# Reordering the transfers at a fused kernel's start, and moving its normalisation pieces within the FFN stages

## Chip, cores, metric

One core of a Trainium2 chip. The metric is device time in microseconds. Each time is the median of a kernel's runs, and the kernel before was run beside every new kernel on the same chip. "Span" is the time from the first to the last instruction of the profiled run; it is 1 to 2 us less than the time. In the profile lines PE is TensorE, PEld its weight loads, DVE VectorE, ACT ScalarE, POOL GpSimd, SP SyncE, and a bracket holds the idle time before an instruction and what ended it. The granted clock is the share of its full rate at which TensorE was let run.

## The reference, cut to what matters

```python
# retention: batch 4, 8 heads, 768 steps, head_dim 64
for t in range(S):
    state = gamma * state + outer(k[:, :, t], v[:, :, t])
    y[:, :, t] = scale * q[:, :, t] @ state
x = y.transpose(0, 2, 1, 3).reshape(3072, 512)
# RMS norm and SwiGLU FFN, d_ff 1536
xn = x / sqrt(mean(x * x) + 1e-6) * rms_g
out = (silu(xn @ w_gate) * (xn @ w_val)) @ w_out
```

## The kernel before

The 768 steps are cut into six chunks of 128. While the FFN of chunk c runs in 16 slots (12 gate/value blocks `gv`, then 4 `down` blocks), the attention pieces of chunk c+1 are put between the slots. Program order is kept on every engine. The chunk's 512 token rows (4 batches of 128) must all have passed through `piece_x` before the next FFN can start.

```python
    for b in range(B):
        load(0, b)                # q, k, v of chunk 0: 12 transfers of 256 KB on SP
    # ... constants, g_bc on SP ...
    for i in range(DFF // WB):    # weights: 8 + 3 transfers on GpSimd, cast to bf16
        nc.gpsimd.dma_start(out=wg_b[:, :, sl], in_=wg_v[:, :, sl])
        nc.gpsimd.dma_start(out=wv_b[:, :, sl], in_=wv_v[:, :, sl])
    # ... wo likewise, 3 transfers ...

    def cast(c, b):               # three GpSimd instructions, then load(c + 1, b)
    def piece_t(c, b):            # transposes of q, k (PE), qkT copy (ACT)
    def piece_a(c, b):            # scores (PE), causal mask am (DVE)
    def piece_y(c, b):            # y, kv (PE); x (DVE); xsq (ACT); state (DVE, POOL)
    def piece_rstd(c):            # once per chunk: two GpSimd instructions
    def piece_x(c, b):
        nc.vector.scalar_tensor_tensor(out=xn, in0=x, scalar=rstd, in1=g_bc, ...)
        for s in range(KS):
            nc.tensor.transpose(xt_ps[:, s, :], xn[:, s * 128:(s + 1) * 128], ident)
        nc.vector.tensor_copy(cur[c, "xnT"][:, :, b * C:(b + 1) * C], xt_ps)

    def attention(c):             # slot of each piece
        for b in range(B):
            s[2 * b].append(lambda b=b: cast(c, b))
            s[2 * b + 1].append(lambda b=b: piece_t(c, b))
            s[2 * b + 2].append(lambda b=b: piece_a(c, b))
            s[2 * b + 3].append(lambda b=b: piece_y(c, b))
            s[12 + b].append(lambda b=b: piece_x(c, b))
        s[10].append(lambda: piece_rstd(c))

    def gv(n):                    # 4 + 4 matmuls of 512 columns
        # g_ps, v_ps (PE), sg = Silu(g_ps) (ACT), hT = sg * v_ps (DVE)
```

Of the kernel before, what the change touches and what calls it, by code (L numbers as in the profile page):

```python
# [9 lines left out]
F32 = mybir.dt.float32  # L10
BF16 = mybir.dt.bfloat16
AX = mybir.AxisListType
AF = mybir.ActivationFunctionType
ALU = mybir.AluOpType
# [3 lines left out]
def kernel(  # L18
# [24 lines left out]
    lng = [math.log(1.0 - 2.0 ** (-5.0 - h)) for h in range(H)]  # L43

    const = ctx.enter_context(tc.tile_pool(name="const", bufs=1))
    loads = ctx.enter_context(tc.tile_pool(name="loads", bufs=5))
    work = ctx.enter_context(tc.tile_pool(name="work", bufs=3))
    ffw = ctx.enter_context(tc.tile_pool(name="ffw", bufs=3))
    aps = ctx.enter_context(tc.tile_pool(name="aps", bufs=4, space=bass.MemoryType.PSUM))
# [2 lines left out]

    out_v = out.rearrange("(b c p) m -> c b p m", b=B, p=C)


    raw = {}

    def load(c, b):
        t = []
        for name, src in (("q_f", q), ("k_f", k), ("v_f", v)):  # L60
            x = loads.tile([128, H, D], F32, name=name)
            nc.sync.dma_start(  # L62
                out=x, in_=src[b].rearrange("h (c p) d -> c p h d", p=C)[c])
            t.append(x)
        raw[c, b] = t

# [22 lines left out]
    for h in range(H):  # L89
        nc.scalar.activation(vdec[:, :, h], pos_f, AF.Exp, scale=-lng[h], bias=zero)  # L90
        nc.scalar.activation(ydec[:, :, h], pos_f, AF.Exp, scale=lng[h], bias=lnscale)
    eps4 = const.tile([128, B], F32, name="eps4")
    nc.gpsimd.memset(eps4, 1e-6)
    mhalf4 = const.tile([128, B], F32, name="mhalf4")
    nc.gpsimd.memset(mhalf4, -0.5)
    g_bc = const.tile([128, DM], F32, name="g_bc")
    nc.sync.dma_start(out=g_bc, in_=moe_rms_g.partition_broadcast(128))

# [11 lines left out]
    wv_v = moe_w_val.rearrange("(k p) n -> p k n", p=128)  # L110
    wo_v = moe_w_out.rearrange("(n p) m -> p n m", p=128)
    WB = 384
    for i in range(DFF // WB):
        sl = slice(i * WB, (i + 1) * WB)
        nc.gpsimd.dma_start(out=wg_b[:, :, sl], in_=wg_v[:, :, sl])
        nc.gpsimd.dma_start(out=wv_b[:, :, sl], in_=wv_v[:, :, sl])
    for i in range(3):
        sl = slice(i * 4, (i + 1) * 4)
        nc.gpsimd.dma_start(out=wo_b[:, sl, :], in_=wo_v[:, sl, :])


    cur = {}

    def cast(c, b):
        q_f, k_f, v_f = raw.pop((c, b))
        qb = work.tile([128, DM], BF16, name="qb")
        kb = work.tile([128, DM], BF16, name="kb")
        vp = work.tile([128, H, D], BF16, name="vp")
        nc.gpsimd.tensor_copy(qb, q_f.rearrange("p h d -> p (h d)"))  # L129
        nc.gpsimd.tensor_copy(kb, k_f.rearrange("p h d -> p (h d)"))  # L130
        nc.gpsimd.tensor_tensor(  # L131
            out=vp, in0=v_f, in1=vdec[:, c, :, None].to_broadcast([128, H, D]), op=ALU.mult)
        cur[c, b] = dict(qb=qb, kb=kb, vp=vp)
        if c + 1 < NCH:
            load(c + 1, b)

    def piece_t(c, b):
# [25 lines left out]
    def piece_y(c, b):  # L163
        d = cur[c, b]
        y_ps = aps.tile([128, H, D], F32, name="y_ps", tag="at")
        first = True
        for hp in range(NHP):
            for i in range(2):
                h = 2 * hp + i
                last = c == 0 and h == H - 1  # L170
                nc.tensor.matmul(y_ps[:, h, :], d["am"][:, i, hp, :], d["vp"][:, h, :],  # L171
                                 start=first, stop=last, skip_group_check=True)
                first = False
        if c > 0:
            for hp in range(NHP):
                nc.tensor.matmul(y_ps[:, 2 * hp:2 * hp + 2, :], d["qT"][:, hp, :], st_b[b][:, hp, :],
                                 start=False, stop=hp == NHP - 1, skip_group_check=True)
        if c < NCH - 1:
            kv_ps = aps.tile([128, NHP, 128], F32, name="kv_ps", tag="at")
            for hp in range(NHP):  # L180
                sl = slice(hp * 128, (hp + 1) * 128)
                nc.tensor.matmul(kv_ps[:, hp, :], d["kb"][:, sl],
                                 d["vp"][:, 2 * hp:2 * hp + 2, :], start=True, stop=True)
        x = work.tile([128, H, D], BF16, name="x", bufs=5)
        nc.vector.tensor_tensor(  # L185
            out=x, in0=y_ps, in1=ydec[:, c, :, None].to_broadcast([128, H, D]), op=ALU.mult)
        xsq = work.tile([128, DM], F32, name="xsq")
        nc.scalar.activation(xsq, x.rearrange("p h d -> p (h d)"), AF.Square,  # L188
                             accum_out=cur[c, "ssq"][:, b:b + 1])
        if c < NCH - 1:  # L190
            for i in range(2):
                r = slice(i * 64, i * 64 + 64)
                kv = kv_ps[r, :, i * 64:i * 64 + 64]
                if c == 0:
                    nc.vector.tensor_copy(st_f[b][r], kv)
                else:
                    nc.vector.tensor_tensor(out=st_f[b][r], in0=st_f[b][r], in1=kv, op=ALU.add)  # L197
                nc.gpsimd.tensor_copy(st_b[b][r, :, i * 64:i * 64 + 64], st_f[b][r])  # L198
        d["x"] = x

    def piece_rstd(c):
        ssq = cur[c, "ssq"]
        ms = work.tile([128, B], F32, name="ms")
        nc.gpsimd.tensor_scalar(out=ms, in0=ssq, scalar1=1.0 / DM, scalar2=1e-6,
                                op0=ALU.mult, op1=ALU.add)
        rstd = work.tile([128, B], F32, name="rstd")
        nc.gpsimd.tensor_tensor(out=rstd, in0=ms, in1=mhalf4, op=ALU.pow)  # L207
        cur[c, "rstd"] = rstd

    def piece_x(c, b):  # L210
        x = cur.pop((c, b))["x"]
        xn = work.tile([128, DM], BF16, name="xn")
        nc.vector.scalar_tensor_tensor(  # L213
            out=xn, in0=x.rearrange("p h d -> p (h d)"), scalar=cur[c, "rstd"][:, b:b + 1],
            in1=g_bc, op0=ALU.mult, op1=ALU.mult)
        xt_ps = aps.tile([128, KS, 128], BF16, name="xt_ps", tag="at")
        for s in range(KS):
            nc.tensor.transpose(xt_ps[:, s, :], xn[:, s * 128:(s + 1) * 128], ident)  # L218
        nc.vector.tensor_copy(cur[c, "xnT"][:, :, b * C:(b + 1) * C], xt_ps)  # L219

    def begin(c):
        cur[c, "ssq"] = work.tile([128, B], F32, name="ssq")
        cur[c, "xnT"] = work.tile([128, KS, GT], BF16, name="xnT", bufs=2)

    def attention(c):

        s = [[] for _ in range(16)]
        s[0].append(lambda: begin(c))
        for b in range(B):
            s[2 * b].append(lambda b=b: cast(c, b))  # L230
            s[2 * b + 1].append(lambda b=b: piece_t(c, b))
            s[2 * b + 2].append(lambda b=b: piece_a(c, b))
            s[2 * b + 3].append(lambda b=b: piece_y(c, b))
            s[12 + b].append(lambda b=b: piece_x(c, b))
        s[10].append(lambda: piece_rstd(c))
        return s


    def ffn(c):
        xnT = cur.pop((c, "xnT"))  # L240
        hT = ffw.tile([128, NFF, GT], BF16, name="hT", bufs=2)
        slots = []

        def gv(n):
            sl = slice(n * 128, (n + 1) * 128)
            g_ps = fps.tile([128, GT], F32, name="g_ps", tag="ff")
            for s in range(KS):
                nc.tensor.matmul(g_ps, wg_b[:, s, sl], xnT[:, s, :], start=s == 0, stop=s == KS - 1)  # L248
            v_ps = fps.tile([128, GT], F32, name="v_ps", tag="ff")
            for s in range(KS):  # L250
                nc.tensor.matmul(v_ps, wv_b[:, s, sl], xnT[:, s, :], start=s == 0, stop=s == KS - 1)  # L251
            sg = ffw.tile([128, GT], BF16, name="sg")
            nc.scalar.activation(sg, g_ps, AF.Silu)  # L253
            nc.vector.tensor_tensor(out=hT[:, n, :], in0=sg, in1=v_ps, op=ALU.mult)  # L254

        def down(b):
            o_ps = fps.tile([128, DM], F32, name="o_ps", tag="ff")
            for n in range(NFF):
                nc.tensor.matmul(o_ps, hT[:, n, b * C:(b + 1) * C], wo_b[:, n, :],  # L259
                                 start=n == 0, stop=n == NFF - 1)  # L260
            o_sb = ffw.tile([128, DM], F32, name="o_sb")
            nc.scalar.copy(o_sb, o_ps)  # L262
            nc.sync.dma_start(out=out_v[c, b], in_=o_sb)

        for n in range(NFF):
            slots.append(lambda n=n: gv(n))
        for b in range(B):
            slots.append(lambda b=b: down(b))
        return slots
# [5 lines left out]
    for c in range(NCH):  # L275
        f_slots = ffn(c)
        a_slots = attention(c + 1) if c + 1 < NCH else [[] for _ in range(16)]
        for i in range(16):
            f_slots[i]()
            for f in a_slots[i]:  # L280
                f()

# [29 lines left out]
```

## Time and profile before

A stage is the stretch from one FFN's first matmul (g_ps) to the next one's.

| kernel before | us |
|---|---|
| first FFN matmul | 59.26 |
| stage 0 (FFN 0, attention 1) | 42.99 |
| stages 1, 2, 3, 4 | 40.47, 40.52, 40.53, 40.30 |
| last stage (FFN 5 alone) | 35.33 |

One more view will be compared later: what TensorE waited for in stage 2 (142.72 to 183.24 us). Its columns are who waited, for whom, us in all, times, longest:

```profile
PE g_ps L248 <- DVE xnT L219: 0.5, 1, 0.5
PE y_ps L171 <- DVE am L158: 0.5, 3, 0.2
PE a_ps L154 <- ACT qkT L144: 0.3, 1, 0.3
```

So TensorE waits 1.3 us in a stage, never more than 0.52 us at a time. The first of these is the stage end, where xn and xnT of the last batch come behind the last down block.

### The profile page before, as it was taken

What the parts mean: (1) busy time and instruction counts of PE and PEld (TensorE: products, weight loads), DVE (VectorE), ACT (ScalarE), POOL (GpSimd) and SP (SyncE); (2) the same over time, 40 slices, a digit from 0 to 9 for tenths busy, and PEclk for the clock granted to TensorE, in tenths of its full rate; (3) what the DMA queues carried; (4) which work ended last, traced back from release to release, by engine and by line L of the source; (5) the groups of instructions that cost most, each with busy time, mean ns of one, the idle gap of its engine ahead of it and who ended that gap; (6) DMA issues with size and microseconds to landing.
All of it is one profiled execution on the core that took longest, in us unless ns stands there. A gap on an engine that the chain in (4) does not pass through costs nothing.

```text
span 299.4 us, 4437 instructions
## 1 busy us (share of the span) xinstructions
PE 242.3 (81%) x1696; PEld 122.8 (41%) x1696; DVE 141.1 (47%) x232; ACT 100.0 (33%) x186; POOL 91.2 (30%) x153
## 2 busy tenths in 40 slices
PE   0025212399999999999999999999999999999994
PEld 0014111145544454544454444545444444544441
DVE  0006405617765266873376653577544556424300
ACT  5012212034452245431445313544224453233321
POOL 8472245403337006281035350161921101000000
PEclk9999999999999999999999999999999999999999
DMA  8999999992400498002793025970110000110012
GB/s 164 191 191 192 196 197 227 219 218 44 96 3 35 129 228 171 2 0 105 182 225 53 0 73 137 219 136 1 36 71 36 2 0 2 70 70 2 1 47 93
DMA packets 84310, 30.43 MB, mean 102 GB/s; under 512 B 75457, under 2 KB 81089, under 8 KB 84289
## 3 DMA queue, kind: packets, MB, share of 16 engines
q1 hardware_dynamic: 78480, 25.43, 41.0%
q0 software_dynamic: 5808, 4.72, 9.8%
q8 instruction: 13, 0.21, 0.3%
q14 instruction: 9, 0.07, 0.1%
HBM read 28.57 MB, written 6.29 MB: 116 GB/s over the span
## 4 chain that ended last, share of the span: by engine, by line
PE 53%; DVE 17%; ACT 9%; SPq 8%; DMA 6%; issue 5%; POOL 1%; DVEq 0%; ACTq 0%; POOLq 0%
PE o_ps L259 21%; PE g_ps L248 13%; PE v_ps L251 12%; SPq L62 8%; DVE am L158 7%; DMA k_f<-in_k_dram 6%; DVE hT L254 4%; ACT xsq L188 3%; DVE x L185 3%; ACT qkT L144 3%; ACT sg L253 3%; PE xt_ps L218 2%; PE y_ps L171 2%; DVE xn L213 1%; DVE xnT L219 1%
## 5 line engine op out<-in xcount | busy, mean ns | idle before, releaser
L254 DVE TENSOR_TENSOR hT<-sg,v_ps 128x512 bf16<-128x512 bf16 x72 | 49.5, 688 | 72.5 <-PE v_ps L251 45.4
L248 PE MATMUL g_ps<-xnT,wg_b 128*128 128x512 bf16 x288 | 75.9, 387 | 3.1 <-DVE xnT L219 3.1
L251 PE MATMUL v_ps<-xnT,wv_b 128*128 128x512 bf16 x288 | 74.9, 383 | 0.0
L259 PE MATMUL o_ps<-wo_b,hT 128*128 128x512 bf16 x288 | 65.6, 379 | 0.0
L253 ACT ACTIVATE sg<-g_ps 128x512 bf16<-128x512 f32 x72 | 43.0, 597 | 63.9 <-PE g_ps L248 63.9
L198 POOL CAST st_b<-st_f 64x256 bf16<-64x256 f32 x40 | 15.9, 397 | 110.6 <-DVE st_f L197 102.5
L158 DVE TENSOR_TENSOR am<-a_ps,causal 128x512 bf16<-128x512 f32 x48 | 30.8, 682 | 33.5 <-PE a_ps L154 33.5
L251 PEld LDWEIGHTS <-wv_b 128*128 128x128 bf16 x288 | 28.5, 99 | 35.0 <-issue 1.7
L259 PEld LDWEIGHTS <-hT 128*128 128x128 bf16 x288 | 27.5, 98 | 30.4
L248 PEld LDWEIGHTS <-wg_b 128*128 128x128 bf16 x288 | 25.5, 99 | 29.1 <-DVE xnT L219 3.5
L262 ACT COPY o_sb<-o_ps 128x512 f32<-128x512 f32 x24 | 14.1, 586 | 56.5 <-PE o_ps L259 56.5
L144 ACT COPY qkT<-qk_ps 128x1024 bf16<-128x1024 bf16 x24 | 23.9, 998 | 25.0 <-PE qk_ps L142 25.0
L188 ACT ACTIVATE xsq<-x 128x512 f32<-128x512 bf16 x24 | 15.1, 630 | 49.4 <-DVE x L185 47.7
L142 PE MATMUL qk_ps<-ident,qb 128*128 128x128 bf16 x96 | 10.2, 234 | 24.4 <-POOL qb L129 24.4
L131 POOL TENSOR_TENSOR vp<-v_f,vdec 128x512 bf16<-128x512 f32 x24 | 26.8, 1117 | 8.7 <-DMA v_f<-in_v_dram 5.5
L219 DVE COPY xnT<-xt_ps 128x512 bf16<-128x512 bf16 x24 | 10.2, 425 | 31.4 <-PE xt_ps L218 31.4
L213 DVE SCALAR_TENSOR_TENSOR xn<-x,rstd,g_bc 128x512 bf16<-128x512 bf16 x24 | 23.5, 980 | 1.9 <-POOL rstd L207 1.9
L129 POOL CAST qb<-q_f 128x512 bf16<-128x512 f32 x24 | 17.0, 707 | 14.4 <-issue 8.8
L171 PE MATMUL y_ps<-vp,am 128*128 128x64 bf16 x192 | 13.6, 202 | 8.7 <-DVE am L158 5.9
L185 DVE TENSOR_TENSOR x<-y_ps,ydec 128x512 bf16<-128x512 f32 x24 | 16.6, 690 | 4.7 <-PE y_ps L171 4.1
L142 PEld LDWEIGHTS <-qb 128*128 128x128 bf16 x96 | 7.1, 105 | 25.8 <-POOL qb L129 24.6
L218 PE MATMUL xt_ps<-ident,xn 128*128 128x128 bf16 x96 | 10.2, 234 | 8.7 <-DVE xn L213 8.7
(38 smaller groups left out, 140.2 us busy)
## 6 DMA issues: line engine op xcount, KB each, us to landing
q_f<-in_q_dram SPq DMA_DIRECT2D x24, 256.0 KB, 4.8
k_f<-in_k_dram SPq DMA_DIRECT2D x24, 256.0 KB, 4.9
v_f<-in_v_dram SPq DMA_DIRECT2D x24, 256.0 KB, 4.9
out_dram<-o_sb SPq DMA_DIRECT2D x24, 256.0 KB, 2.0
wg_b<-in_moe_w_gate_dram POOLq DMA_DIRECT2D x4, 384.0 KB, 13.4
wv_b<-in_moe_w_val_dram POOLq DMA_DIRECT2D x4, 384.0 KB, 15.5
wo_b<-in_moe_w_out_dram POOLq DMA_DIRECT2D x3, 512.0 KB, 23.0
g_bc<-in_moe_rms_g_dram SPq DMA_DIRECT2D x1, 256.0 KB, 8.1
```

The costliest lines, as they stand in the source:

```text
L62: nc.sync.dma_start(out=x, in_=src[b].rearrange("h (c p) d -> c p h d", p=C)[c])
L131: nc.gpsimd.tensor_tensor(out=vp, in0=v_f, in1=vdec[:, c, :, None].to_broadcast([128, H, D]), op=ALU.mult)
L144: nc.scalar.copy(qkT, qk_ps)
L158: nc.vector.tensor_tensor(out=am[:, i], in0=a_ps[i], in1=causal[:, None, :].to_broadcast([128, NHP, 128]), op=ALU.mult)
L185: nc.vector.tensor_tensor(out=x, in0=y_ps, in1=ydec[:, c, :, None].to_broadcast([128, H, D]), op=ALU.mult)
L188: nc.scalar.activation(xsq, x.rearrange("p h d -> p (h d)"), AF.Square, accum_out=cur[c, "ssq"][:, b:b + 1])
L213: nc.vector.scalar_tensor_tensor(out=xn, in0=x.rearrange("p h d -> p (h d)"), scalar=cur[c, "rstd"][:, b:b + 1], in1=g_bc, op0=ALU.mult, o ...
L248: nc.tensor.matmul(g_ps, wg_b[:, s, sl], xnT[:, s, :], start=s == 0, stop=s == KS - 1)
L251: nc.tensor.matmul(v_ps, wv_b[:, s, sl], xnT[:, s, :], start=s == 0, stop=s == KS - 1)
L253: nc.scalar.activation(sg, g_ps, AF.Silu)
L254: nc.vector.tensor_tensor(out=hT[:, n, :], in0=sg, in1=v_ps, op=ALU.mult)
L259: nc.tensor.matmul(o_ps, hT[:, n, b * C:(b + 1) * C], wo_b[:, n, :], start=n == 0, stop=n == NFF - 1)
```

## The change

Its intent is an earlier start: chunk 0's loads have the DMA engines to themselves, the weights follow, the second chunk's loads follow the first FFN blocks, and chunk 0's casts are shared out. It also makes rstd per batch and moves the x pieces forward, for every chunk. Core of the diff:

```diff
-    loads = ctx.enter_context(tc.tile_pool(name="loads", bufs=5))
+    loads = ctx.enter_context(tc.tile_pool(name="loads", bufs=6))
+    nc.scalar.activation(warm, zero, AF.Silu)
 ... cast(c, b):
-        nc.gpsimd.tensor_copy(qb, ...)
-        nc.gpsimd.tensor_copy(kb, ...)
+        if c == 0:
+            nc.scalar.copy(qb, ...)
+            nc.vector.tensor_copy(kb, ...)
+        else: ... both on gpsimd
+        if c == 0 and b == 2:
+            load_w(0)
+        if c == 0 and b == 3:
+            ... load_w(1), load_w(2), load_w(3), load_wo(0..2)
-        if c + 1 < NCH:
+        if 0 < c < NCH - 1:
             load(c + 1, b)
 ... piece_y: ssq and rstd per batch, [128, 1] instead of [128, 4] once per chunk
+    PLAN = dict(cast=(0, 2, 4, 6), t=(1, 3, 5, 7), a=(2, 4, 6, 8), y=(3, 5, 7, 9), x=(6, 8, 10, 12))
+    PLAN1 = dict(cast=(6, 7, 9, 11), t=(7, 9, 11, 13), a=(8, 10, 12, 14), y=(9, 11, 13, 15), x=(11, 13, 15, 15))
+        plan = PLAN1 if c == 1 else PLAN
 ... main loop, FFN of chunk 0:
+            if c == 0 and i in (1, 2, 3, 4):
+                load(1, i - 1, after=mark[0, i])   # mark: the Silu of block i
```

More of the change, by code (lines that the diff above doesn't have):

```diff
@@ L53, with load @@
     out_v = out.rearrange("(b c p) m -> c b p m", b=B, p=C)
+    SYNC_DEP = mybir.DependencyInfo(mybir.DependencyClass.Sync, mybir.DependencyReason.DATA)
     raw = {}
-    def load(c, b):
+    def load(c, b, after=None):
         t = []
@@ L61, in load @@
             x = loads.tile([128, H, D], F32, name=name)
-            nc.sync.dma_start(
+            i = nc.sync.dma_start(
                 out=x, in_=src[b].rearrange("h (c p) d -> c p h d", p=C)[c])
+            if after is not None:
+                tc.add_manual_dep(i.ins, after.ins.name, SYNC_DEP, reason="transfer order")
             t.append(x)
@@ L91 @@
         nc.scalar.activation(ydec[:, :, h], pos_f, AF.Exp, scale=lng[h], bias=lnscale)
-    eps4 = const.tile([128, B], F32, name="eps4")
-    nc.gpsimd.memset(eps4, 1e-6)
-    mhalf4 = const.tile([128, B], F32, name="mhalf4")
-    nc.gpsimd.memset(mhalf4, -0.5)
+    mhalf = const.tile([128, 1], F32, name="mhalf")
+    nc.gpsimd.memset(mhalf, -0.5)
+    warm = const.tile([128, 1], F32, name="warm")
+    nc.scalar.activation(warm, zero, AF.Silu)
     g_bc = const.tile([128, DM], F32, name="g_bc")
@@ L112, with load_w @@
     WB = 384
-    for i in range(DFF // WB):
+    def load_w(i):
         sl = slice(i * WB, (i + 1) * WB)
@@ L116, with load_wo @@
         nc.gpsimd.dma_start(out=wv_b[:, :, sl], in_=wv_v[:, :, sl])
-    for i in range(3):
+    def load_wo(i):
         sl = slice(i * 4, (i + 1) * 4)
@@ L122 @@
     cur = {}
+    mark = {}
     def cast(c, b):
@@ L128, in cast @@
         vp = work.tile([128, H, D], BF16, name="vp")
-        nc.gpsimd.tensor_copy(qb, q_f.rearrange("p h d -> p (h d)"))
-        nc.gpsimd.tensor_copy(kb, k_f.rearrange("p h d -> p (h d)"))
+        if c == 0:
+            nc.scalar.copy(qb, q_f.rearrange("p h d -> p (h d)"))
+            nc.vector.tensor_copy(kb, k_f.rearrange("p h d -> p (h d)"))
+        else:
+            nc.gpsimd.tensor_copy(qb, q_f.rearrange("p h d -> p (h d)"))
+            nc.gpsimd.tensor_copy(kb, k_f.rearrange("p h d -> p (h d)"))
         nc.gpsimd.tensor_tensor(
@@ L133, in cast @@
         cur[c, b] = dict(qb=qb, kb=kb, vp=vp)
-        if c + 1 < NCH:
+        if c == 0 and b == 2:
+            load_w(0)
+        if c == 0 and b == 3:
+            for i in range(1, DFF // WB):
+                load_w(i)
+            for i in range(3):
+                load_wo(i)
+        if 0 < c < NCH - 1:
             load(c + 1, b)
@@ L187, in piece_y @@
         xsq = work.tile([128, DM], F32, name="xsq")
+        ssq = work.tile([128, 1], F32, name="ssq")
         nc.scalar.activation(xsq, x.rearrange("p h d -> p (h d)"), AF.Square,
-                             accum_out=cur[c, "ssq"][:, b:b + 1])
+                             accum_out=ssq)
         if c < NCH - 1:
@@ L199, in piece_y, with piece_rstd @@
         d["x"] = x
-    def piece_rstd(c):
-        ssq = cur[c, "ssq"]
-        ms = work.tile([128, B], F32, name="ms")
-        nc.gpsimd.tensor_scalar(out=ms, in0=ssq, scalar1=1.0 / DM, scalar2=1e-6,
+        d["ssq"] = ssq
+        piece_rstd(c, b)
+    def piece_rstd(c, b):
+        ms = work.tile([128, 1], F32, name="ms")
+        nc.gpsimd.tensor_scalar(out=ms, in0=cur[c, b]["ssq"], scalar1=1.0 / DM, scalar2=1e-6,
                                 op0=ALU.mult, op1=ALU.add)
-        rstd = work.tile([128, B], F32, name="rstd")
-        nc.gpsimd.tensor_tensor(out=rstd, in0=ms, in1=mhalf4, op=ALU.pow)
-        cur[c, "rstd"] = rstd
+        rstd = work.tile([128, 1], F32, name="rstd")
+        nc.gpsimd.tensor_tensor(out=rstd, in0=ms, in1=mhalf, op=ALU.pow)
+        cur[c, b]["rstd"] = rstd
     def piece_x(c, b):
-        x = cur.pop((c, b))["x"]
+        d = cur.pop((c, b))
         xn = work.tile([128, DM], BF16, name="xn")
         nc.vector.scalar_tensor_tensor(
-            out=xn, in0=x.rearrange("p h d -> p (h d)"), scalar=cur[c, "rstd"][:, b:b + 1],
+            out=xn, in0=d["x"].rearrange("p h d -> p (h d)"), scalar=d["rstd"],
             in1=g_bc, op0=ALU.mult, op1=ALU.mult)
@@ L221, in begin @@
     def begin(c):
-        cur[c, "ssq"] = work.tile([128, B], F32, name="ssq")
         cur[c, "xnT"] = work.tile([128, KS, GT], BF16, name="xnT", bufs=2)
+    PLAN = dict(cast=(0, 2, 4, 6), t=(1, 3, 5, 7), a=(2, 4, 6, 8), y=(3, 5, 7, 9), x=(6, 8, 10, 12))
+    PLAN1 = dict(cast=(6, 7, 9, 11), t=(7, 9, 11, 13), a=(8, 10, 12, 14), y=(9, 11, 13, 15), x=(11, 13, 15, 15))
     def attention(c):
@@ L228, in attention @@
         s[0].append(lambda: begin(c))
+        plan = PLAN1 if c == 1 else PLAN
+        pieces = dict(cast=cast, t=piece_t, a=piece_a, y=piece_y, x=piece_x)
         for b in range(B):
-            s[2 * b].append(lambda b=b: cast(c, b))
-            s[2 * b + 1].append(lambda b=b: piece_t(c, b))
-            s[2 * b + 2].append(lambda b=b: piece_a(c, b))
-            s[2 * b + 3].append(lambda b=b: piece_y(c, b))
-            s[12 + b].append(lambda b=b: piece_x(c, b))
-        s[10].append(lambda: piece_rstd(c))
+            for n, f in pieces.items():
+                s[plan[n][b]].append(lambda f=f, b=b: f(c, b))
         return s
@@ L252, in gv @@
             sg = ffw.tile([128, GT], BF16, name="sg")
-            nc.scalar.activation(sg, g_ps, AF.Silu)
+            mark[c, n] = nc.scalar.activation(sg, g_ps, AF.Silu)
             nc.vector.tensor_tensor(out=hT[:, n, :], in0=sg, in1=v_ps, op=ALU.mult)
```

## The prediction

> **What bounds the kernel now.** I read the page first, then the chain of waits in order of time, then the engines' busy time by stage, then single stretches in order of time. Columns of the chain: start us, length us, what.
>
> ```profile
> 16.91 7.11 SPq L62
> 24.07 17.99 DMA k_f<-in_k_dram
> 42.18 0.62 POOL kb L130
> ...
> 49.51 1.06 POOL rstd L207
> 50.59 1.10 DVE xn L213
> ...
> 59.26 1.86 PE g_ps L248 x4
> ```
>
> The first FFN matmul (g_ps, FFN of chunk 0) runs at 59.26 us. Up to 42 us the chain is nothing but the loads of chunk 0: issues on SP stretched to 7 us, then an 18 us landing. The DMA engines are busy all that time, because the weights go out at 4 to 18 us and share them (columns of the DMA windows: stretch, its length, PE, PEld, DVE, ACT, POOL busy, clock, DMA share, GB/s):
>
> ```profile
> 2.00:4.00 2.00, 0.00 (x0) 0.00 (x0) 0.00 (x0) 1.73 (x10) 1.96 (x9) 1.00 1.05 233
> 8.00:10.00 2.00, 0.00 (x0) 0.00 (x0) 0.00 (x0) 0.00 (x0) 2.00 (x4) 1.00 1.28 192
> ```
>
> Loads alone move 233 GB/s, one of 256 KB per 1.1 us; beside the weights a load's issue takes 4.2 us at 12.71 us, so the loads get some 62 of the 192 GB/s. After 59 us TensorE is the bound. Stages from one FFN's first matmul to the next:
>
> ```profile
> 59.26:102.25 42.99, 41.70 (x288) 20.51 (x287) 23.86 (x40) 15.61 (x28) 13.89 (x22) 1.00 0.43 84
> 142.72:183.24 40.52, 39.15 (x288) 19.96 (x289) 23.84 (x40) 15.61 (x28) 13.89 (x22) 1.00 0.48 105
> 264.07:299.40 35.33, 31.25 (x144) 14.02 (x144) 8.26 (x12) 9.51 (x16) 0.00 (x0) 1.00 0.10 38
> ```
>
> A stage is 40.5 us, 39.15 of it PE busy: 1.4 us of slack. The first has 43.0, since its first matmuls run at half rate (1.86 us for four, later 0.86). What decides the effect of the moved x pieces is slot 6 of a stage (start, length, engine and line):
>
> ```profile
> 158.24 1.03 PE L251 MATMUL v_ps<-xnT,wv_b 128*128 128x512 bf16 x4
> 158.26 0.99 ACT L144 COPY qkT<-qk_ps 128x1024 bf16<-128x1024 bf16 x1
> 159.15 0.60 ACT L253 ACTIVATE sg<-g_ps 128x512 bf16<-128x512 f32 x1
> 159.31 0.40 PE L154 MATMUL a_ps<-qkT 64*128 64x128 bf16 x8
> 159.78 0.69 DVE L254 TENSOR_TENSOR hT<-sg,v_ps 128x512 bf16<-128x512 bf16 x1 [1.41 <-ACT sg L253]
> ...
> 172.18 1.63 DVE L213 SCALAR_TENSOR_TENSOR xn<-x,rstd,g_bc 128x512 bf16<-128x512 bf16 x1
> ...
> 174.66 0.74 DVE L213 SCALAR_TENSOR_TENSOR xn<-x,rstd,g_bc 128x512 bf16<-128x512 bf16 x1
> ```
>
> PE is through with slot 6's FFN block at 159.1 and goes straight to a_ps. DVE reaches that block's hT only at 159.78, because ACT did xsq and qkT before the Silu. So DVE runs 1.3 us behind PE here, and each engine keeps program order.
>
> **What the Trainium skill says.** "DMA: Bandwidth & Descriptors", Queues, rings and completion order: each DMA engine goes round-robin over the queue rows with work, by packets. The trace agrees in kind: both queues share one total of about 190 GB/s. "SBUF — State Buffer", Who interferes with whom: a VectorE instruction with two SBUF inputs and a GpSimd one that reads SBUF block each other for a whole instruction. Trace: the same xn takes 0.74 us alone, 1.63 beside vp on POOL. "TensorE: Matmul & The Clock Gate", Part 1: the array falls to half rate after an idle window of about 3.4 us and needs about as long of work to recover; here the slow matmuls at 59.26 us last about 5 us. "ScalarE activation tables: per-element evaluation and per-set limits" puts one table load at 1283 ns; the trace has 1.28 us at 48.73, hidden there.
>
> **Part 1, the start (gain).** Loads of chunk 0 alone: q0 lands at 4.1 us as now, then one per 1.13 us: v3 at about 16.6. I then walked the twelve loads through the new order with durations of the trace. ACT has 16 Exp until 5.4, the early Silu table load to 6.7, then qb 0.6 (estimate from the copies). T0 at 7.4, qkT 1.0, a 0.65, am 1.3: y0 at 11.2. A batch takes 5.05 us now where no load holds it (18.98 to 24.08); with an x piece in it, xn 0.74 and xnT 0.42 come ahead of am on DVE, so 5.9: y1 16.4, y2 22.7, y3 28.5. POOL issues block 0 of the weights from 16 us, vp3 at 20.4, then nine issues of 0.77 us, 21.4 to 28.3; today the ninth outstanding weight transfer waits for the first to land, which by then has. Only then come st_b, ms and rstd of batches 2 and 3 (0.9+0.2+1.0 each): rstd3 at 32.5. xn, transposes and xnT (1.1 with xt, 0.5 more, waits in it) end at 34.5. **First FFN matmul at 34.6 instead of 59.3: minus 24.7 us.** The four rstd in place of one also put POOL on this path.
>
> Weights: 4.72 MB as written at about 160 GB/s (the software queue's 9.8% of the span is 29 us of all 16 engines): block 0 landed at 23.5, then 4.9 us a block, 38 for the last, wo at 48 to 51. Needed at 34.6, 42.5, 48, 53 and about 63: hidden.
>
> **Part 2, stage 0 (loss).** Loads of chunk 1 wait for the Silu of blocks 1 to 4, so begin near 40.7 us, get some 40 GB/s until wo is in, then 230: batches in at 50, 54, 57, 60.5. PLAN1 wants them at slots 6, 7, 9, 11, that is 48 to 59 us: at most 1 us of stall. x0 in slot 11 costs 1.8 us (as in part 3). The end is worse: y3 and x3 both stand in slot 15 behind the last down block. Their serial path is y 0.9, x 0.7, xsq 0.8, st_b, ms 0.2, pow 1.05, xn 0.74, xt 0.6, xnT 0.4, with the hops between them what 46.01 to 52.8 shows now: about 6 us with PE idle, where the old end of the stage has 0.7. Sum: +1.8 +5.5, less 1 for waits that vanish: **stage 0 43.0 to 49.3, +6.3.** An idle of over 3.4 us can also make the next matmuls cold; the first time it cost 2.7 us, I take half: **+1.5.**
>
> **Part 3, stages 1 to 4 (loss).** The x pieces move from slots 12 to 15, where DVE is idle, to 6, 8, 10, 12. In slot 6 PE must do xt before a_ps; xt needs xn, xn stands behind hT on DVE. hT ends 160.47 on today's clock, xn 161.2 to 161.5 (POOL's casts are beside it), xt then: PE would have gone on at 159.1 to 159.3. That is 2.1 us of stall. Slot 8 the same, 2.0 (its own qkT and am waits of 0.2 and 0.16 disappear in it, so 1.8 net). Slot 10: Silu 10 also follows an xsq, but no qkT: hT starts 2.0 us after the block, so 1.7, and pow of batch 3 may hold xn up to 0.6 longer. The 0.22 us of each xt only moves. Given back: the wait at the stage end, 0.7. Sum: 2.1+1.8+1.9-0.6 = **5.2 us a stage, four stages: +20.8.** Extra rstd work on POOL (three more pairs of 1.2 us a stage) delays the casts from 153.45 to about 154.7, still ahead of qk_ps at 156.93: nothing.
>
> **Sum.** 299.4 - 24.7 + 6.3 + 1.5 + 20.8 = 303.3 of span, about 304 as timed (span 299.4 ran as 300.4). Last stage: untouched.
>
> **Rivals.** (a) The mid-stage stall isn't there, for instance because DVE has the time for xn before hT: then stages 1 to 4 each lose the 0.7 at the end, and the kernel is 299.4-24.7+7.8-2.8 = 280. For it: DVE is only 24 of 40.5 us busy. Against: its order is the program's in every stretch I read (hT, then am, also where a_ps was ready before hT). (b) Weights too late: if DVE's work holds up the weight issues on POOL, or loads and weights share worse, stage 0 waits for wo or chunk 1 and the time is 305 to 312. For it: 62 us of DMA work (16+29+16) stand ahead of a stage that ends near 84. Against: each need above has 5 us or more, chunk 1's loads excepted. (c) POOL not on the start path (weights out earlier): first matmul near 31, total 300.
>
> **Range and chances.** Two large terms nearly cancel, each good to 3 to 5 us. I am least sure of the size of the stalls, which can only be smaller if DVE or ACT run ahead, and of the start. A schedule so detailed was likely kept for some reason, so I go a little below my sum: 302, range 288 to 312. Faster by over 2% (below 294.4): 0.24; within 2%: 0.47; slower: 0.29.
>
> **What would show it.** First g_ps near 34.6 us with POOL's weight issues right before the late rstd; a PE gap of 5 to 6 us just before stage 1's first g_ps, maybe slow matmuls after it; in stages 1 to 4 three PE waits of about 2 us each on xn (line of xt_ps), stage length 45 to 46, no gap at the stage end. Wrong if stages 1 to 4 stay at 40 us, or if the first FFN matmul comes before 30 or after 39 us.

## More of the kernel before

Times of the kernel before: 300.41 us (299.94 to 301.83), the median of the three runs at hand before the prediction; with a fourth run it is 300.71.

## The result, and the profile after

310.21 us (309.92 to 311.0) against 300.71 us: the ratio is 1.0317 (95% interval 1.0278 to 1.0357), slower. A ratio here is the mean time of one kernel's runs over that of the other's of the same rounds, so not quite the ratio of the medians quoted. The measured time is inside the predicted range, in the outcome (slower) that had been given 0.29.

| | before | after | difference | predicted difference |
|---|---|---|---|---|
| first FFN matmul | 59.26 | 34.40 | -24.86 | -24.7 |
| stage 0 | 42.99 | 47.96 | +4.97 | +6.3 |
| stage 1 | 40.47 | 49.73 | +9.26 | +6.7 (5.2 and 1.5 cold) |
| stages 2 to 4 | 121.35 | 141.93 | +20.58 | +15.6 |
| last stage | 35.33 | 35.28 | -0.05 | 0 |
| span | 299.4 | 309.3 | +9.9 | +3.9 |

The start came as worked out. The chain of the changed kernel at its start (start us, us, what) has no load left in it; it ends in xn and transposes:

```profile
30.77 0.76 POOL st_b L218
32.47 0.76 DVE xn L234
33.28 0.62 PE xt_ps L239 x4
35.20 1.06 PE g_ps L269 x2
```

The POOL timeline (start, length, engine, line, operation, idle before) shows the last weight issues standing ahead of batch 2's state cast and rstd:

```profile
26.30 2.28 POOL L126 DMA_DIRECT2D wo_b<-in_moe_w_out_dram  x3
28.50 0.94 POOL L218 CAST st_b<-st_f 64x256 bf16<-64x256 f32 x2
29.53 0.19 POOL L225 TENSOR_SCALAR ms<-ssq 128x1 f32<-128x1 f32 x1
29.80 0.56 POOL L228 TENSOR_TENSOR rstd<-ms,mhalf 128x1 f32<-128x1 f32 x1
```

Then the stages (columns as in the prediction). The second is stage 2; its window begins 0.17 us after that stage's first matmul (132.09 us), with the same length. The clock column, third from the end, is what had not been foreseen there:

```profile
34.40:82.36 47.96, 41.33 (x283) 20.87 (x288) 23.65 (x40) 15.90 (x28) 17.17 (x31) 0.98 1.10 211
132.26:179.40 47.14, 40.10 (x284) 20.54 (x288) 23.15 (x40) 15.60 (x28) 15.84 (x28) 0.96 0.42 90
```

What TensorE waited for in stage 2 after the change:

```profile
PE xt_ps L239 <- DVE xn L234: 6.0, 3, 2.3
PE g_ps L269 <- issue: 0.5, 3, 0.2
PE a_ps L173 <- ACT qkT L163: 0.3, 1, 0.3
PE y_ps L190 <- DVE am L177: 0.2, 1, 0.2
```

Three waits on xn, 6.0 us, where all waits came to 1.3. The wait on xnT at the stage end is gone. Slot 6 of stage 1, in order of time, shows the first of the three, and TensorE's lines behind it show what follows:

```profile
100.50 1.03 PE L272 MATMUL v_ps<-xnT,wv_b 128*128 128x512 bf16 x4
100.58 0.99 ACT L163 COPY qkT<-qk_ps 128x1024 bf16<-128x1024 bf16 x1
101.47 0.60 ACT L274 ACTIVATE sg<-g_ps 128x512 bf16<-128x512 f32 x1
102.10 0.69 DVE L275 TENSOR_TENSOR hT<-sg,v_ps 128x512 bf16<-128x512 bf16 x1 [1.47 <-ACT sg L274]
102.71 1.03 DVE L234 SCALAR_TENSOR_TENSOR xn<-x,rstd,g_bc 128x512 bf16<-128x512 bf16 x1
103.80 0.40 PE L239 MATMUL xt_ps<-ident,xn 128*128 128x128 bf16 x4 [2.27 <-DVE xn L234]
...
105.85 1.91 PE L272 MATMUL v_ps<-xnT,wv_b 128*128 128x512 bf16 x4
```

TensorE stands for 2.27 us, since xn waits for hT on VectorE, hT for the Silu and the Silu for qkT. After that the four v_ps matmuls take 1.91 us instead of 1.03. One microsecond of that stretch in the windows view has the granted clock at 0.50:

```profile
106.00:107.00 1.00, 1.00 (x4) 0.31 (x3) 0.00 (x0) 0.60 (x1) 0.00 (x0) 0.50 0.00 0
```

It is back at full rate at 108.20 us. In stages 2, 3 and 4 the same happens behind the second wait, in slot 8 (2.19, 2.19 and 2.42 us long), but not behind the first, in slot 6 (2.27, 2.58 and 3.01 us): length alone does not decide it. The part after e10 comes back to this.

The end of stage 0 is as foreseen: xt of the last batch waits 3.89 us for its xn, which waits for y, x, xsq and rstd of the same batch. Stage 1 then starts at half rate:

```profile
81.23 0.61 PE L239 MATMUL xt_ps<-ident,xn 128*128 128x128 bf16 x4 [3.89 <-DVE xn L234]
...
84.02 1.91 PE L272 MATMUL v_ps<-xnT,wv_b 128*128 128x512 bf16 x4
```

### The profile page after: what moved, and what is told of

It is laid out like the page before. It is cut to its first block, busy times and chain, and to the rows that moved or that the text cites. A ratio compares the mean times of both kernels' runs of the same rounds, so it can differ in the third digit from the quotient of the medians.

```text
span 309.3 us, 4472 instructions
## 1 busy us (share of the span) xinstructions
PE 248.0 (80%) x1666; PEld 126.5 (41%) x1696; DVE 139.7 (45%) x236; ACT 102.4 (33%) x191; POOL 97.3 (31%) x180
## 4 chain that ended last, share of the span: by engine, by line
PE 62%; DVE 17%; ACT 9%; issue 6%; POOL 4%; DVEq 0%; ACTq 0%; POOLq 0%
PE o_ps L280 20%; PE g_ps L269 17%; PE v_ps L272 16%; DVE xn L234 5%; DVE x L204 4%; DVE hT L275 3%; DVE am L177 3%; PE xt_ps L239 3%; ACT qkT L163 3%; ACT xsq L208 2%; PE a_ps L173 2%; ACT sg L274 2%; PE y_ps L190 1%; PE qk_ps L161 1%; POOL rstd L228 1%
## 5 line engine op out<-in xcount | busy, mean ns | idle before, releaser
L272 PE MATMUL v_ps<-xnT,wv_b 128*128 128x512 bf16 x284 | 79.1, 402 | 0.3
L269 PE MATMUL g_ps<-xnT,wg_b 128*128 128x512 bf16 x269 | 76.9, 401 | 2.6 <-issue 1.1
L280 PE MATMUL o_ps<-wo_b,hT 128*128 128x512 bf16 x281 | 63.8, 379 | 0.4
L218 POOL CAST st_b<-st_f 64x256 bf16<-64x256 f32 x40 | 16.7, 418 | 102.8 <-DVE st_f L217 97.9
L272 PEld LDWEIGHTS <-wv_b 128*128 128x128 bf16 x288 | 29.6, 103 | 38.4 <-issue 7.8
L280 PEld LDWEIGHTS <-hT 128*128 128x128 bf16 x288 | 27.8, 98 | 32.3
L269 PEld LDWEIGHTS <-wg_b 128*128 128x128 bf16 x288 | 26.6, 101 | 28.8 <-issue 5.6
L143 POOL TENSOR_TENSOR vp<-v_f,vdec 128x512 bf16<-128x512 f32 x24 | 27.6, 1150 | 6.2 <-DMA v_f<-in_v_dram 6.2
L239 PEld LDWEIGHTS <-xn 128*128 128x128 bf16 x96 | 6.5, 104 | 45.8 <-DVE xn L234 44.4
L234 DVE SCALAR_TENSOR_TENSOR xn<-x,rstd,g_bc 128x512 bf16<-128x512 bf16 x24 | 20.2, 841 | 2.3 <-POOL rstd L228 2.1
L141 POOL CAST qb<-q_f 128x512 bf16<-128x512 f32 x20 | 13.4, 669 | 14.0 <-PE v_ps L272 14.0
```

Source lines behind the costliest of these rows:

```text
L143: nc.gpsimd.tensor_tensor(out=vp, in0=v_f, in1=vdec[:, c, :, None].to_broadcast([128, H, D]), op=ALU.mult)
L234: nc.vector.scalar_tensor_tensor(out=xn, in0=d["x"].rearrange("p h d -> p (h d)"), scalar=d["rstd"], in1=g_bc, op0=ALU.mult, op1=ALU.mult)
L269: nc.tensor.matmul(g_ps, wg_b[:, s, sl], xnT[:, s, :], start=s == 0, stop=s == KS - 1)
L272: nc.tensor.matmul(v_ps, wv_b[:, s, sl], xnT[:, s, :], start=s == 0, stop=s == KS - 1)
L280: nc.tensor.matmul(o_ps, hT[:, n, b * C:(b + 1) * C], wo_b[:, n, :], start=n == 0, stop=n == NFF - 1)
```

## The experiments

**Theory.** The transfers' new order gains 24 us. The x pieces in the middle of a stage lose it: TensorE waits in its own order for an xn that is queued behind hT (about 5 us a stage), and the waits then drop its clock (about 2 us a stage). **Rivals.** The extra rstd work on GpSimd costs the time; VectorE has no room in mid-stage; the slow matmuls aren't caused by the waits; the start's gain comes from the casts on three engines.

Stages from each trace, in us:

| kernel | first FFN matmul | stage 0 | 1 | 2 | 3 | 4 | time |
|---|---|---|---|---|---|---|---|
| before | 59.26 | 42.99 | 40.47 | 40.52 | 40.53 | 40.30 | 300.4 |
| after | 34.40 | 47.96 | 49.73 | 47.14 | 47.40 | 47.39 | 310.21 |
| e1 | 34.44 | 46.18 | 42.31 | 40.65 | 40.91 | 40.42 | 284.10 |
| e2 | 34.43 | 47.97 | 43.99 | 41.36 | 41.65 | 41.87 | 287.71 |
| e3 | 34.45 | 46.80 | 47.70 | 45.66 | 45.94 | 46.18 | 304.67 |
| e4 | 58.44 | 46.87 | 51.19 | 45.66 | 47.44 | 47.63 | 334.29 |
| e5 | 34.20 | 47.28 | 49.60 | 47.11 | 47.11 | 47.62 | 309.15 |
| e6 | 34.87 | 41.59 | 40.64 | 40.64 | 40.93 | 40.41 | 276.03 |
| e7 | 33.67 | 49.76 | 39.95 | 39.94 | 40.22 | 39.73 | 279.75 |
| e8 | 37.10 | 46.14 | 50.70 | 45.65 | 47.40 | 47.47 | 313.12 |
| e9 | 34.44 | 41.74 | 39.96 | 39.94 | 40.24 | 39.73 | 273.23 |
| e10 | 34.97 | 47.38 | 40.62 | 40.63 | 40.93 | 40.42 | 281.33 |

The changed kernel, e1, e2 and e3 are the same program up to the end of stage 0, yet that stage lasts 46.18 to 47.97 us: matmuls at half rate fill its beginning for 2.4 us in e1 and for 5.5 us in the changed kernel. A difference of up to 1.8 us in stage 0 is not an edit's.

**e1_late_x.** From chunk 2 on the x pieces return to slots 12 to 15.

```diff
+    PLAN2 = dict(PLAN, x=(12, 13, 14, 15))
-        plan = PLAN1 if c == 1 else PLAN
+        plan = PLAN1 if c == 1 else PLAN2 if c > 1 else PLAN
```

> One part undone: from chunk 2 on the x pieces go back to slots 12 to 15; everything else as in the changed kernel. Theory (xt on TensorE waits for an xn that stands behind hT on VectorE, and the idle TensorE then runs at half rate for a while): the three waits of about 2 us and the half-rate spells vanish, stages 2 to 4 go from 47.3 to 40.5 us, stage 1 from 49.9 to about 43 (it keeps 2.7 of cold start), total near 310 - 27 = 283. Rival 1 (the four rstd pairs on GpSimd, or other new work, cost the time): stages stay at 45 or more, total above 300.

Measured: 284.10 us, ratio to before 0.944 (0.9394 to 0.9485). Stages 2 to 4 are back within 0.4 us of the old ones, though each still has four rstd pairs, so these cost at most that. The waits on xn are gone. This one plan line is worth 26 us.

**e2_split.** xn stays in mid-stage, only its transposes and xnT come a slot later.

```diff
+        d["xn"] = xn
+
+    def piece_xt(c, b):
+        xn = cur.pop((c, b))["xn"]
         ... transposes and xnT copy ...
+    PLAN2 = dict(PLAN, xt=(7, 9, 11, 13))
```

> From chunk 2 on xn stays in slots 6, 8, 10, 12 but its transposes and xnT move one slot later (7, 9, 11, 13). The same VectorE work stays in the middle of the stage. Theory (it is TensorE's place in its own order that costs, not VectorE's load): waits on xn below 0.5 us, stages 2 to 4 at 40 to 41.5, total 281 to 286. Rival 2 (VectorE has no room in the middle of a stage): stages stay at 44 or more, total above 297.

Measured: 287.71 us, ratio 0.9568 (0.9533 to 0.9603), 1.7 us above the top of what was expected; stages 0 and 1 of its profiled run have the longer half-rate beginnings. Stage 2 lasts 41.36 us at granted clock 1.00; the long waits are gone with the same VectorE work in the same stretch. What TensorE waits for in its stage 2, by the same view (0.2 us of other waits left out):

```profile
PE y_ps L190 <- DVE am L177: 1.2, 4, 0.4
PE a_ps L173 <- ACT qkT L163: 0.5, 2, 0.3
```

So the place in TensorE's order is the cause, and VectorE's load a small part of it: am comes up to 0.4 us late because xn now lies ahead of it, 0.7 us more than in e1 in stages 2 and 3, and 1.45 us in stage 4, where xt still waits up to 0.46 us for xn.

**e3_fill.** The changed kernel with TensorE kept busy in the waits.

```diff
+        for j in range((24, 24, 18, 0)[b] if c > 1 else 0):
+            nc.tensor.transpose(xt_ps[:, j % KS, :], ident, ident)
         for s in range(KS):
             nc.tensor.transpose(xt_ps[:, s, :], xn[:, s * 128:(s + 1) * 128], ident)
```

> The changed kernel, plus 24, 24 and 18 idle transposes of the identity on TensorE (about 1.3 and 1.0 us, into the buffer that xt then overwrites) ahead of xt of batches 0, 1 and 2 from chunk 2 on. The waits for xn stay as they are, only TensorE is not idle in them. Theory with the clock gate: granted clock 1.0 in stages 2 to 4 (now 0.96), each of them 1.7 to 2.2 us shorter (about 45.3), total near 302.5. If the half-rate spells have no part in it: 310, or a little more.

Measured: 304.67 us, ratio 1.0136 (1.0101 to 1.0172). Work that does nothing makes the kernel 5.5 us faster. Stage 2 in the windows view:

```profile
128.95:174.61 45.66, 42.18 (x350) 23.91 (x355) 23.18 (x40) 15.59 (x28) 15.88 (x28) 1.00 0.47 93
```

The clock is 1.00 and the stage 1.48 us shorter; stages 3 and 4 gain 1.46 and 1.21, below the 1.7 to 2.2 expected. Stage 1 gains 2.03, in part because 4.16 us of it instead of 5.36 are its slow beginning. What is left against e1's stage 2 (45.66 - 40.65 = 5.0 us) is the waits themselves, the 5.2 of the prediction. This splits the loss of such a stage: some 5.0 us of waiting, 1.2 to 1.5 us of half-rate matmuls.

**e4_weights_first.** Only the weights' order is undone.

```diff
+    ... load_w(0..3), load_wo(0..2) ahead of the main loop, as before
-        if c == 0 and b == 2:
-            load_w(0)
-        if c == 0 and b == 3:
-            ... load_w(1..3), load_wo(0..2)
```

> Undoes the order of the weight transfers alone (they are issued at the program's start again); casts on three engines and early x pieces stay. Theory: chunk 0's loads again land at about 42 us, the first FFN matmul comes at 51 to 54 us (the x pieces of batches 0 to 2 no longer stand behind the last batch, which before cost some 7 us), later stages unchanged but stage 0 perhaps 2 us shorter, total near 327. If the order hardly mattered and the casts did it: first matmul below 42 us.

Measured: 334.29 us, ratio 1.1125 (1.1087 to 1.1162). The first FFN matmul comes at 58.44 us. So 24.0 of the 24.9 us of the start come with the transfers' order, given the other parts. The expected 51 to 54 us was wrong, and the VectorE timeline shows why:

```profile
43.69 0.75 DVE L232 SCALAR_TENSOR_TENSOR xn<-x,rstd,g_bc 128x512 bf16<-128x512 bf16 x1 [13.96 <-DMA g_bc<-in_moe_rms_g_dram]
```

The early xn of batch 0 needs g_bc, which is queued behind all twelve loads. Once batch 0's x piece stands ahead of batch 2's scores, this wait holds up batches 2 and 3 too. So the early piece, which had been expected to bring 5 to 8 us here, brings 0.8 (58.44 against 59.26).

**e5_casts_pool.** The casts of chunk 0 on GpSimd again.

```diff
-        if c == 0:
-            nc.scalar.copy(qb, ...)
-            nc.vector.tensor_copy(kb, ...)
-        else:
-            nc.gpsimd ...
+        nc.gpsimd.tensor_copy(qb, ...)
+        nc.gpsimd.tensor_copy(kb, ...)
```

> The changed kernel with only the casts of chunk 0 put back on GpSimd. Theory (the start is set by the loads' landing, the chain from scores to xn, and GpSimd's weight issues ahead of the late rstd, not by the casts): first FFN matmul between 33.5 and 36 us (34.4 now), total within 1.5 us of 310. If the three-engine casts carried a part of the gain: first matmul at 37 us or later.

Measured: 309.15 us, ratio 1.0291 (1.0244 to 1.0338); first FFN matmul at 34.20 us. The casts on three engines bring nothing that can be measured. The early Silu and the sixth load buffer were not tried apart; in the chain of the changed kernel the table load of that Silu takes 1.28 us from 5.49 us on.

**e6_plan1.** e1, with the second chunk's plan moved up.

```diff
-    PLAN1 = dict(cast=(6, 7, 9, 11), t=(7, 9, 11, 13), a=(8, 10, 12, 14), y=(9, 11, 13, 15), x=(11, 13, 15, 15))
+    PLAN1 = dict(cast=(6, 7, 8, 9), t=(7, 9, 10, 11), a=(8, 10, 11, 12), y=(9, 11, 12, 13), x=(12, 13, 14, 15))
```

> On top of e1_late_x the second chunk's plan is moved up (casts at slots 6, 7, 8, 9; y at 9, 11, 12, 13; x at 12 to 15). Theory (the end of stage 0 is y3 and x3 in one slot, 3.9 us of wait on xn, then a cold TensorE): the wait is at most 0.7 us, no slow matmuls at stage 1's start, the 1.5 us wait of x0 in slot 11 is gone; stage 0 near 41.5, stage 1 near 40.6, total 274 to 277. Rival (chunk 1's loads land too late for the earlier casts): the waits reappear ahead of its transposes and the total stays at 281 or more.

Measured: 276.03 us, ratio 0.9188 (0.9139 to 0.9238). Stage 0 is 41.59 us and stage 1 starts at full rate. The loads are there in time.

**e7_best.** e6 with two more edits.

```diff
+    PLAN2 = dict(PLAN, x=(10, 11, 12, 13), xt=(12, 12, 13, 14))
 ... weight blocks 2, 3 and wo are issued after the rstd of batch 3 of chunk 0
```

> On top of e6: from chunk 2 on xn at slots 10 to 13 and its transposes at 12, 12, 13, 14, so that nothing is left at the stage end; weight blocks 2 and 3 and wo are issued behind the last rstd of chunk 0. Theory: first FFN matmul near 32.3 instead of 34.4, stages 1 to 4 near 40 (the 0.7 us at the end gone), total 269 to 273. If late weights hold up stage 0, a wait ahead of g_ps or o_ps shows there and the total is above 274.

Measured: 279.75 us, ratio 0.9306 (0.9262 to 0.935), slower than e6. The plan does what was expected (stages 1 to 4 near 40.0). The FFN starts at 33.67 us, 1.2 us earlier than in e6 but not at the expected 32.3, and stage 0 grows by 8.2 us. What waits isn't an FFN matmul, as feared, but the transposes of chunk 1's q and k:

```profile
50.81 0.40 PE L156 MATMUL qk_ps<-ident,qb 128*128 128x128 bf16 x4 [1.90 <-POOL qb L141]
54.58 0.61 PE L156 MATMUL qk_ps<-ident,kb 128*128 128x128 bf16 x4 [3.37 <-POOL kb L142]
```

The casts wait for chunk 1's loads: one of 256 KB takes 6.21 us to issue at 39.39 us, beside the late weights, whose last lands at 53.26 us. Half-rate matmuls follow from 53.32 to 60.15 us. So the weights have to be out of the way of chunk 1's loads too.

**e8_no_mark.** Chunk 1's loads without the waits on the Silu.

```diff
-                load(1, i - 1, after=mark[0, i])
+                load(1, i - 1)
```

> The changed kernel without the waits of chunk 1's loads on the Silu of the first FFN blocks: they go out right behind g_bc, beside the weights. Estimate from the shares seen before (loads 40 to 62 GB/s beside the weights): weight block 0 lands near 25 us, block 3 near 45, wo near 58, needed at 34, 50 and 61: nothing waits for long, total within 2 us of 310. If the order of these loads is worth something: waits ahead of g_ps in stage 0 and a total of 313 or more.

Measured: 313.12 us, ratio 1.0419 (1.0358 to 1.0479), some 3 us above the changed kernel. The FFN waits for no weight, as estimated, but the first FFN matmul comes at 37.10 us. GpSimd's last wo issue is held up until an earlier weight transfer has landed, and the late rstd stands behind it:

```profile
30.21 0.74 POOL L126 DMA_DIRECT2D wo_b<-in_moe_w_out_dram  x1 [2.04 <-DMA wg_b<-in_moe_w_gate_dram]
```

The issue waits for the semaphore of the third weight transfer (113), which it uses itself: the program has eight such counters for GpSimd's transfers and takes them in turn, so that the ninth to eleventh issues wait for the first to third landings. The waits on the Silu are thus worth 2.7 us, by a way that I hadn't thought of.

**e9_combo.** e6 with e7's PLAN2 and the weights in the order of the changed kernel.

> e6 with the split of e7 alone (xn of chunks 2 to 5 at slots 10 to 13, transposes at 12, 12, 13, 14), the weights in the order of the changed kernel. Theory: stages 1 to 4 near 40.0 as in e7, start and stage 0 as in e6 (34.9 and 41.6), so e6 less 4 times 0.65: total 273 to 274, the fastest. If the two do not add: 276.

Measured: 273.23 us (272.55 to 273.57), ratio 0.9092 (0.9056 to 0.9128). It beats both kernels.

**e10_fill_end.** e1 with TensorE kept busy ahead of the last xt of chunk 1.

```diff
+        for j in range(60 if (c, b) == (1, 3) else 0):
+            nc.tensor.transpose(xt_ps[:, j % KS, :], ident, ident)
```

> e1 plus 60 idle transposes of the identity (3.3 us) on TensorE in the 3.9 us wait ahead of the last xt of chunk 1, at the end of stage 0. The wait keeps its length. Theory (an idle stretch is what drops the clock): no half-rate matmuls at stage 1's start, stage 1 near 40.6 instead of 42.3, total 1.5 to 2 us below e1, near 282. If idleness is not the cause: matmuls of 0.43 us at stage 1's start as in e1 and 284.

Measured: 281.33 us, ratio 0.9354 (0.9317 to 0.9391). Stage 1 falls from 42.31 to 40.62 us, and its first matmuls run at full rate. TensorE's lines at that place:

```profile
77.38 3.51 PE L239 MATMUL xt_ps<-ident 128*128 128x128 bf16 x60
81.43 0.40 PE L241 MATMUL xt_ps<-ident,xn 128*128 128x128 bf16 x4 [0.54 <-DVE xn L234]
82.35 1.02 PE L273 MATMUL g_ps<-xnT,wg_b 128*128 128x512 bf16 x4 [0.52 <-DVE xnT L242]
```

The four g_ps take 1.02 us at once; in the changed kernel they came slow after the same wait. So it is idleness that drops the clock. The two totals are of different calls, and the two profiled runs have the same span (280.2 us), since e10's stage 0 begins with the longer slow stretch; the stage is the better measure.

**Which waits drop the clock.** The traces settle more than the lines above use. In each run all changes of the granted clock lie whole multiples of 3.41 us apart (changed kernel: 39.93, 80.89, 87.72, 104.78, 108.20, 159.40 us, that is 12, 2, 5, 1 and 15 steps). Cut into these steps, from the first one at full rate to just before the last matmul, the twelve traces have 825 steps at full rate. All 23 in which TensorE was idle for 1.99 us or more were followed by half rate, none of those with 1.84 us or less, and one of the four between 1.90 and 1.93. So a wait of 2.3 us drops the clock only if nearly all of it falls into one step, which no edit here aimed at. In e4 and e8 stage 2 has waits of 2.27, 2.20 and 1.73 us and no drop; here is e8's:

```profile
133.94:179.59 45.65, 39.02 (x290) 19.96 (x289) 23.15 (x40) 15.59 (x28) 15.83 (x28) 1.00 0.45 93
```

It lasts as long as in e3, which confirms the 5.0 us of waiting without idle transposes. Their stage 1 has two drops. The loss to half rate is thus partly chance, run by run; the loss to waiting is not.

## Why the prediction was right or wrong

The range held the result and the mechanism was right except for one term, but the centre was 8 us low. It held because it was 24 us wide; the missing term alone is 6 us.

- **The start, -24.7 us**: right (-24.86), by the steps given. One term was mis-sized with little effect: rstd for one column takes 0.55 us, not 1.0, and a longer st_b (1.20 us) and the hops make up for most of it. The casts, which the walk put on the path, turned out to be worth nothing (e5).
- **Stage 0, +6.3 us**: measured +4.97. The wait ahead of the last xt was 3.89 us plus the xt and xnT behind it, and x0's wait in slot 11 was 1.52 us. With the second chunk's plan moved up both all but go (0.29 us is left), and stage 0 lasts 41.59 us (e6).
- **Stages 1 to 4, 5.2 us each**: here the sum fails. The waits were right: 6.0 us by the profile, 5.0 net by e3 against e1. What was missing is the half rate after one wait of each stage. That term was set to zero, because the prediction counted on a drop only after an idle window of about 3.4 us, and no single wait was that long; about 2 us of idleness in one 3.41 us step was enough. It was 1.2 to 1.5 us in each of stages 2 to 4 (e3), and 6.2 us with stage 1, whose 2.03 hold some of the slow beginning.
- **The cold start of stage 1, taken as half of 2.7**: it came in full in the profiled run, where the half rate lasted two steps (80.89 to 87.72 us). In e1 it lasted one (81.16 to 84.58) and cost 1.7 us (42.31 against 40.62 in e10), so its size varies from run to run.
- **The shading**: the sum was about 304 as timed, and I put 302 because such a schedule "was likely kept for some reason". The trace gave no ground for it; without it the error would have been 6 us. The step from span to time was short as well: the profiled run with the span of 299.4 us was timed at 301.07, so the sum as timed is 305.
- **Readings**: the xn of 0.74 us was not alone: vp on GpSimd began 0.14 us after it and took 1.50 us instead of 1.04. There GpSimd waited, in the 1.63 us case VectorE; the sums don't change. The batch of 18.98 to 24.08 is 5.10 us, not 5.05, and 16+29+16 is 61.
- Rival (a), VectorE does xn before hT, fell: hT comes first in every stage. Rival (b), weights or loads too late, didn't occur in the changed kernel, but did in e7. Rival (c), a start near 31 us, did not occur.

So the gain was real and was given back elsewhere. The change belongs to chunk 0, whose attention runs alone, and its new plan was applied to all chunks. With the x pieces back in their old slots from chunk 2 on (e1) the same transfers give 0.944, and with the second chunk's plan mended too 0.9188.

## What to carry to other kernels

A piece that ends on TensorE should be placed by when its input leaves the engine ahead of it, in that engine's own order, and not by how busy that engine is on average; splitting the producer from the consumer by one slot took stage 2 from 47.14 to 41.36 us here (e2). When a wait on TensorE can't be avoided, count the slow matmuls that may follow it as well as its length, and read their cost from more than one run. A schedule that is good where a stage runs alone should be tried apart where it runs beside other work.

## What the Trainium skill lacked or had wrong

- "TensorE: Matmul & The Clock Gate", Part 1, "HAM oscillation": its rule is to have no idle gaps above about 3.4 us. The page's next section has frequent short idles bring the drop too, but gives no size. Here one wait of 2.19 to 2.42 us in each of stages 1 to 4 of the changed kernel was followed by 3.4 us at granted clock 0.50. In all twelve traces 1.99 us of idleness or more within one 3.41 us step was followed by half rate, and 1.84 us or less was not. Cutting the waits to 0.7 to 0.9 us by idle transposes kept the clock at 1.00 in stage 2.
- "DMA: Bandwidth & Descriptors", Queues, rings and completion order: it has the queues taking turns by packets, but not what share each gets. Loads in 256-byte rows got about 40 to 62 of 190 GB/s beside the weights (a load's issue took 4.2 to 7.1 us instead of 1.1).
- No page has it that with eight weight transfers outstanding on GpSimd the ninth waits for the first to land, and holds up all later work of GpSimd (2.04 us on one issue in e8). By the trace this is the program's doing, not shown to be a limit of the chip: the ninth issue waits for and reuses the first one's semaphore (107 in the kernel before).
- No page gives the time of a pow on GpSimd: 1.01 us for 128x4, 0.55 us for 128x1.
